# P times V of the 8-key units in 64-key pieces on two row halves of the array

## The chip, the cores and the metric

The kernel runs on one NeuronCore of a Trainium2 chip. The core has a matrix engine (TensorE, "PE" in the profile, with its weight loads as "PEld"), VectorE ("DVE"), ScalarE ("ACT"), GpSimd ("POOL") and SyncE ("SP"); each works through its own instructions in order and waits on semaphores for the others. Matrix products land in PSUM, an accumulator memory of eight banks of 512 floats per partition. The metric is the device time of one execution in microseconds (us), lower is better.

## The reference

Two attention layers work on separate inputs, and their outputs are put side by side. Both have 2048 tokens, width 1024 and 32 heads of 32. Layer B sees the last 256 keys. Layer A sees 8 keys, each two tokens apart:

```python
W, dil = 8, 2
qkv = (x @ wqkv) ...                       # q, k, v of 32 heads
idx = pos[:, None] - off[None, :]          # off = arange(8) * 2
logits = einsum("bhsd,bhswd->bhsw", q, kg) * scale     # masked where idx < 0
o = einsum("bhsw,bhswd->bhsd", softmax(logits), vg)
return o.reshape(B, S, D) @ wo
```

The kernel takes A's even tokens and its odd tokens as two sequences of 1024, in which a query sees itself and the seven keys before it.

## The kernel before, in words

The work is cut into eight units of 512 tokens. Units 0 to 3 are layer B ("dense" in the code), units 4 to 7 are layer A ("window" in the code). Units 1, 2, 3, 5 and 7 continue a sequence, so that they need keys of the unit ahead of them; the code calls this a halo. A unit works through eight groups of four heads. For each group there is the product of the projections q and k (`qk_items`, the matmuls of L576), in some places a product for v (`v_items`, L641), and later the output projection (`o_items`, L702). These are the general matmuls. Each is done in three terms of split operands: a high part and a low part of each float, hence the splitting of weights on ScalarE or VectorE (L216, L219, L222) all through the kernel.

A group of a window unit (`window`, L741) goes through these steps.

1. `scores` (L772): for each of four blocks of 128 keys, for each 64-key half of a block and for each of the four heads, a matmul of 64 keys by 72 queries with a contraction of 32. The outputs go to four PSUM banks of the ring `rs`, one for each head. The item is ready only when all four banks of the ring are free (`rs.empty()`), and when the group two before it is done with its buffers.
2. `mask`, `top`, `expo`, `total` (L780 to L808): softmax on VectorE and ScalarE, in a tile `band`.
3. Transposes in 32 by 32 blocks (L811) and `spread` (L820, L823): ScalarE puts the pieces into a tile `wide`, where each head has, for each block of 128 keys, a stretch of 136 queries. What no key sees there is zero.
4. `values` (L838): P times V. For each block and head a matmul with the 128 keys as contraction, the 32 columns of V as stationary operand, and the 136 queries of the block as moving operand (128 in the last block); with a halo, 8 queries more against the last block of the unit before. Heads go to four quarters of the partitions of one PSUM bank, the only one of the ring `ro`. Blocks overlap in 8 queries and are accumulated there.
5. `finish` (L883): ScalarE copies the bank as the high part of the output (L888), and VectorE later subtracts to get the low part (L892). Then the bank is given back.

The order of all instructions is set when the kernel is built. A planner (`Clock` and the loop at the end of the kernel) keeps an estimated time for each engine. It goes through four lists of items (`aux`, `twos` with second scores and values, `ones` with first scores, `gemm` with the general matmuls) and always issues the one that can start first by these estimates. An item has a ready time, a price in us of TensorE's time, and an `after` that issues the following work of other engines. The price of `scores` is `CW` = 0.75, that of `values` is `C3 + 0.9` = 1.1. Work put off with `ck.defer` is issued when the planned time of TensorE has reached the time given. A ring gives a bank out by `take` and gets it back by `give` with a planned time.

The dense units have their own scores (L923, L1005) and values (L1052); they also end in `finish`.

Of the kernel before, what the change touches and what calls it, by code (L numbers as in the profile page):

```python
# [7 lines left out]
F32 = mybir.dt.float32  # L8
F32R = mybir.dt.float32r
AF = mybir.ActivationFunctionType  # L10
ALU = mybir.AluOpType
# [3 lines left out]
P = 128  # L15
NG = 8
NK = 8
S = 512
# [8 lines left out]
LAG7, LAG0 = 1, 3  # L27
TAIL = 4
C1, C3, CG, CV = 0.108, 0.2, 0.231, 0.242
CW = 0.75  # L30
ORDER = (0, 1, 2, 3, 4, 5, 6, 7)
PACE = ((0.1, 1.2, 0.1, 0.0, 0.0, -99, 2), (0.2, 1.2, 0.0, 0.0, 0.2, -99, 1), (0.2, 1.2, 0.0, 0.0, 0.0, -99, 2), (0.2, 0.6, 0.0, 0.0, 0.2, -99, 2), (4.0, 7.0, 0.5, 0.0, 1, 2), (4.0, 7.0, 1.5, 0.5, 1, 1), (4.0, 7.0, 0.5, 0.2, 1, 3), (4.0, 7.0, 0.5, 0.0, 1, 2))
V_AT = ({1: 0, 3: 1, 7: 2}, {0: 0, 5: 1, 7: 2}, {0: 0, 5: 1, 7: 2}, {0: 0, 5: 1, 7: 2}, {0: 0, 5: 1, 7: 2}, {0: 0, 6: 1, 7: 2}, {0: 0, 5: 1, 7: 2}, {0: 0, 5: 1, 7: 2})
# [210 lines left out]
def kernel(ctx, tc, xs, wqk, wv, wo, outs, units):  # L244


    nc = tc.nc
# [17 lines left out]
    ck = Clock()  # L265


    def parts_of(u):
        return VPARTS if len(V_AT[u]) == 3 else VPARTS_LATER
# [40 lines left out]
    for p in plan:  # L310
# [3 lines left out]
        elif p[0] == "v":  # L314
            if slots_of(p[1]).get(NG - 1) == p[2] and p[1] + 1 < U:
                continue
            s0, n = parts_of(p[1])[p[2]]
# [10 lines left out]
        else:  # L328
            u = p[1] - 1
# [8 lines left out]
    for key, i in where.items():  # L338
        u = min(key[1] + (key[0] == "o"), U - 1)
# [3 lines left out]
    st = Stream(nc, ck, raws, wpool, xpool, items, [more[:, 1024 * i:1024 * i + 1024] for i in range(3)],  # L343
                light)
# [65 lines left out]
    band, wide, turned = [None, None], [None, None], [None, None]  # L410
# [3 lines left out]
    xt, xready, ot, rows = {}, {}, {}, {}  # L414
    done, waiting = {}, {}
# [26 lines left out]
    rg, rs, ro = Ring(psg, 7 - NS, "g"), Ring(pss, NS, "s"), Ring(pso, 1, "o")  # L442
# [7 lines left out]
    def latest(*ts):  # L450
        return None if any(t is None for t in ts) else max(ts)
# [278 lines left out]
    def x_items(u):  # L730
        xt[u], xready[u] = [], []

        def run(g):
            a, b = st.get(where["x", u, g])
            xt[u] += a
            xready[u] += b

        return [[(lambda: 0.0, lambda g=g: run(g), 0.0, lambda: None)] for g in range(4)]


    def window(u, s):  # L741


        has_halo = units[u][3]
        buf = s % 2
        hg = u * NG + s
        vp, vc = vparts[parts_of(u)][s]
        v = vbufs[parts_of(u)][vp]
# [4 lines left out]
        def p16():  # L753
            return band[buf][:, :1536].rearrange("p (i c) -> p i c", c=96)[:, :, 24:]

        kbs = [(-1, 0, 8)] if has_halo else []
        kbs += [(0, 0, 136), (1, 128, 136), (2, 256, 136), (3, 384, 128)]
        h = {}

        def scores_ready():  # L760
# [67 lines left out]
        def values_ready():  # L828
            if st.next_holds() is not None and (st.next_holds(), NG - 1) not in done["out"]:
                return None  # L830
            return latest(done["v"].get((u, vp)), h.get("p"), ro.when())

        def values():
            h["o"], _ = ro.take()
            for n, (kb, q0, w) in enumerate(kbs):
                c = 136 * kb + 8 if kb >= 0 else 0
                for j in range(4):
                    nc.tensor.matmul(h["o"][32 * j:32 * j + 32, q0:q0 + w],  # L838
                                     v[:, (4 * u + kb) % 6, vc + 32 * j:vc + 32 * j + 32], wide[buf][:, j, c:c + w],
                                     start=(n == 0), stop=(n == len(kbs) - 1), skip_group_check=True)  # L840

            def after():
                finish(u, s, h)

            return after

        return [Item(scores_ready, scores, CW)], [Item(values_ready, values, C3 + 0.9)]

    def free_keys(hg):

# [32 lines left out]
    def finish(u, s, h):  # L883
        hg = u * NG + s
        done["o"][hg] = ck.now
        o = st.tile(u)
        ot[u, s] = o
        nc.scalar.copy(o[:, 0, :], h["o"])  # L888
        r = ck.use("act", 0.485, ck.now + ck.SEM)

        def low():
            nc.vector.tensor_tensor(o[:, 1, :], h["o"], o[:, 0, :].bitcast(F32), op=ALU.subtract)  # L892
            e = ck.use("dve", 0.61, r)
            ro.give(0, e)
            done["ot"][hg] = e

        ck.defer(r, low)


    def attention(u, s):  # L900
        dense, has_halo = units[u][2], units[u][3]
        if not dense:
            return window(u, s)
# [174 lines left out]
    for u in range(U):  # L1078
        for s in range(NG):
            a, b = attention(u, s)  # L1080
# [15 lines left out]
    for p in plan:  # L1096
        if p[0] == "qk":
            new = qk_items(p[1], p[2])
            if p == ("qk", 0, 0):
                q, k, x = new[:NK], new[NK:], x_items(0)  # L1100
# [16 lines left out]
    n = TAIL  # L1117
# [11 lines left out]
    if WARM:  # L1129
        idle = qst[1][:, 0, :]  # L1130
        nc.vector.memset(idle.bitcast(F32), 0.0)
        ps, bank = rs.take()
# [77 lines left out]
```

## Time and profile before

| | |
|---|---|
| timed runs | 1805.52, 1805.71 and 1807.08 us |
| median of them | 1805.71 us |
| profiled execution, first to last instruction (span) | 1803.3 us |
| TensorE busy | 1788.7 us (99%) |
| VectorE busy | 1229.5 us (68%) |
| ScalarE busy | 1036.7 us (57%) |
| GpSimd busy | 386.9 us (21%) |
| granted TensorE clock | 1.000 |

The profiled execution is known by its span; the timed runs are 2.2 to 3.8 us longer than it. In the profile's lists, a group of instructions is named by its line in the kernel, its engine and operation, the tile written and the tile read, and the shape. Behind the count stand the busy time of the group, the mean duration of one in ns, and the idle time of the engine just ahead of them with what ended it. The ends of matmuls are modelled, and matmuls overlap each other, so what an item takes of TensorE is better read from starts: from its first matmul to the first matmul of the next item. A matmul of plain floats stands as two records.

### The profile page before, as it was taken

The numbers are of one execution on the slowest core, as the hardware profiler recorded it, in microseconds if no ns is written. First come the engines' busy times: TensorE is split into PE (matmuls) and PEld (weight loads), VectorE is DVE, ScalarE is ACT, GpSimd is POOL, SyncE is SP. The second block draws the span as 40 slices with busy tenths as digits, with TensorE's granted clock in tenths as the row PEclk, the third lists the DMA queues.
The fourth block names the chain that finished last, engine by engine and source line by source line (L and its number), as shares of the span: only waits on it lengthen the run. The fifth ranks groups of instructions, "written<-read, shape, count | busy, mean of one in ns | idle before, by whom it ended". The sixth has DMA issues, their size and how long they took to land.

```text
span 1803.3 us, 34584 instructions
## 1 busy us (share of the span) xinstructions
PE 1788.7 (99%) x12778; PEld 1462.7 (81%) x12778; DVE 1229.5 (68%) x2631; ACT 1036.7 (57%) x2643; POOL 386.9 (21%) x905
## 2 busy tenths in 40 slices
PE   8999999999999999999999999999999999999999
PEld 6787877888787788787888788878888888888887
DVE  6677875657766668666676486686677566866673
ACT  5667667665766665766677364453445344634452
POOL 3222223232232223323233300110001100100000
PEclk9999999999999999999999999999999999999999
DMA  8355665545546455554544433433334443533332
GB/s 243 115 151 136 184 167 148 170 130 172 160 135 177 139 152 176 139 155 134 153 137 138 128 125 125 140 126 135 128 112 151 142 135 113 159 129 135 126 105 82
DMA packets 109129, 257.20 MB, mean 143 GB/s; under 512 B 14496, under 2 KB 29856, under 8 KB 108960
## 3 DMA queue, kind: packets, MB, share of 16 engines
q0 software_dynamic: 41760, 152.06, 26.6%
q1 hardware_dynamic: 56832, 83.00, 17.3%
q10 hardware_dynamic: 10368, 19.93, 3.0%
q8 instruction: 101, 1.65, 0.4%
q14 instruction: 68, 0.56, 0.1%
HBM read 164.63 MB, written 23.07 MB: 104 GB/s over the span
## 4 chain that ended last, share of the span: by engine, by line
PE 94%; DMA 2%; ACT 2%; DVE 2%; issue 0%; POOL 0%; ACTq 0%; SPq 0%; DVEq 0%
PE g L576 38%; PE g L702 19%; PE g L641 18%; PE s L1005 6%; PE s L923 5%; PE o L1052 5%; PE o L838 2%; PE s L772 1%; DMA kst<-nat 1%; DMA halo<-nat 1%; ACT qst L968 1%; DVE s L928 0%; DVE w L222 0%; DMA raw<-xs 0%; ACT kst L391 0%; DMA qst<-nat 0%
## 5 line engine op out<-in xcount | busy, mean ns | idle before, releaser
L576 PE MATMUL g<-x,w 128*128 128x512 f32 x3072 | 763.7, 393 | 2.4 <-ACT x L216 1.3
L576 PEld LDWEIGHTS g<-x,w 128*128 128x128 f32 x3072 | 567.1, 188 | 111.5 <-issue 3.2
L641 PE MATMUL g<-w,x 128*128 128x256 f32 (+1 forms) x2304 | 390.0, 320 | 1.3 <-DVE w L222 1.2
L928 DVE CUSTOM_DVE_ANT_0 s<-s,mask_d 128x384 f32<-128x384 f32 (+2 forms) x512 | 263.2, 553 | 153.5 <-PE s L923 152.3
L222 DVE TENSOR_TENSOR w<-raw,w 128x512 fp32r<-128x512 f32 x516 | 336.6, 694 | 41.1 <-ACT w L216 34.6
L641 PEld LDWEIGHTS g<-w,x 128*128 128x128 f32 x2304 | 333.0, 190 | 30.6 <-DVE w L222 3.2
L702 PE MATMUL g<-ot,w 128*128 128x512 f32 x1416 | 344.0, 393 | 0.9 <-ACT ot L888 0.7
L933 ACT ACTIVATE s<-s,nm 128x384 f32<-128x384 f32 (+2 forms) x512 | 273.5, 535 | 75.0 <-DVE nm L928 72.7
L702 PEld LDWEIGHTS g<-ot,w 128*128 128x128 f32 x1416 | 261.8, 188 | 56.1 <-issue 1.8
L991 POOL TENSOR_SCALAR_AFFINE_SELECT pbuf<-pbuf 128x128 f32<-128x128 f32 (+1 forms) x574 | 205.9, 386 | 267.7 <-ACT pbuf L1012 263.7
L1012 ACT ACTIVATE pbuf<-s 128x384 f32<-128x384 f32 (+2 forms) x480 | 199.5, 506 | 54.7 <-PE s L1005 51.7
L219 DVE CAST w<-raw 128x1024 fp32r<-128x1024 f32 x189 | 130.8, 692 | 76.7 <-PE g L576 44.4
L166 POOL DMA_DIRECT2D raw<-wqk x126 | 68.7, 545 | 458.9 <-DVE w L222 315.8
L923 PE MATMUL s<-kst,qst 96*128 96x384 f32 (+2 forms) x512 | 144.5, 342 | 2.2 <-DMA kst<-nat 1.8
L1005 PEld LDWEIGHTS s<-qst,kst 128*128 128x128 f32 x704 | 108.9, 189 | 36.0 <-ACT s L933 13.2
L1005 PE MATMUL s<-qst,kst 128*128 128x256 f32 (+2 forms) x704 | 132.1, 303 | 1.4 <-ACT qst L968 1.0
L820 ACT COPY wide<-wide 32x256 f32<-32x256 f32 x256 | 103.4, 404 | 38.3 <-DVE wide L811 34.9
L923 PEld LDWEIGHTS s<-kst,qst 96*128 96x128 f32 x512 | 92.4, 188 | 27.2 <-issue 8.1
L166 POOL DMA_DIRECT2D raw<-wv x72 | 46.4, 644 | 279.7 <-DVE w L222 167.9
L933 ACT ACTIVATION_READ_ACCUMULATOR s<-s,nm 128x1 f32 x512 | 104.7, 205 | 0.2
L166 POOL DMA_DIRECT2D raw<-wo x64 | 36.1, 564 | 295.2 <-DVE w L222 158.2
L594 ACT COPY ost<-g 128x512 f32<-128x512 f32 x44 | 25.8, 586 | 120.2 <-PE g L702 120.2
(79 smaller groups left out, 1399.4 us busy)
## 6 DMA issues: line engine op xcount, KB each, us to landing
raw<-wqk POOLq DMA_DIRECT2D x126, 512.0 KB, 3.7
raw<-wv POOLq DMA_DIRECT2D x72, 512.0 KB, 4.2
raw<-wo POOLq DMA_DIRECT2D x64, 512.0 KB, 3.9
qst<-nat SPq DMA_DIRECT2D x96, 256.0 KB, 3.8
kst<-nat SPq DMA_DIRECT2D x96, 256.0 KB, 4.0
raw<-xs POOLq DMA_DIRECT2D x28, 512.0 KB, 4.5
outs<-ost ACTq DMA_DIRECT2D x56, 256.0 KB, 2.2
kst<-halo SPq DMA_DIRECT2D x72, 128.0 KB, 2.7
```

The lines of the kernel that those rows point to most:

```text
L166: (self.nc.scalar if early else self.nc.gpsimd).dma_start(raw if len(ap.shape) == 2 else raw.rearrange("p (a b) -> p a b", a=2), ap)
L219: nc.vector.tensor_copy(t[:, 0, :], raw)
L222: nc.vector.tensor_tensor(t[:, 1, c:c + 512], raw[:, c:c + 512], t[:, 0, c:c + 512].bitcast(F32), op=ALU.subtract)
L576: nc.tensor.matmul(h["ps"], h["w"][:, a, k * P:(k + 1) * P], xt[u][k][:, b, :], start=(k == 0 and i == 0), stop=(k == NK - 1 and i == 2))
L641: nc.tensor.matmul(ps, xt[u][kw * g + k][:, a, p0:p0 + P], h["w"][g][:, c, k], start=(first and t == 0 and half == 0), stop=(last and t == 2),
L702: nc.tensor.matmul(h["ps"], w[:, a, c:c + P], ot[u, k][:, b, :], start=(k == 0 and i == 0), stop=(k == NK - 1 and i == 2))
L923: nc.tensor.matmul(ps[:, :n], q[0:96, j, b * P:(b + 1) * P], kk[0:96, j, c0:c1], start=True, stop=True)
L928: nc.vector.tensor_tensor_reduce(ps[:, :n], ps[:, :n], mask[:, cut:full], scale=-1.0, scalar=BIG, op0=ALU.add, op1=ALU.min, accum_out=nm)
L933: nc.scalar.activation(ps[:, :n], ps[:, :n], AF.Exp, bias=nm, scale=-1.0, accum_out=sm)
L991: nc.gpsimd.affine_select(w, w, pattern=[[0, m], [step, n]], compare_op=ALU.is_ge, fill=0.0, base=base, channel_multiplier=chan)
L1005: nc.tensor.matmul(ps[:, i * n:(i + 1) * n], kk[:, j, 256 + kb * P:256 + (kb + 1) * P], q[:, j, q0:q0 + n], start=True, stop=True)
L1012: nc.scalar.activation(w, ps[:, :pack * n].rearrange("p (j n) -> p j n", j=pack), AF.Exp)
```

## The change

Only units 4 to 7 are edited. In `values` each 128-key block is taken in two pieces of 64 keys. A piece is a matmul with a contraction of 64, on the lower or the upper 64 rows of the array, with 72 queries as moving operand (64 for the last piece). The lower pieces are accumulated in the bank of `ro`, as before; the upper pieces go to a second bank, one of the four of the ring `rs`, which `values` now waits for and takes. A halo is one more piece of 8 queries for each head on the upper rows.

Every bank holds 72 queries of each 128, so the two banks overlap in 8 queries of each 64. A new `join` takes the place of `finish`: ScalarE copies the first 8 columns of every 64 of the upper bank to an unused part of `band`; VectorE adds them to the lower bank; ScalarE copies columns 72 to 127 of each 128 from the upper bank and columns 0 to 71 from the lower one as the high part; VectorE subtracts, later, in the same two portions. The upper bank is given back after the first subtraction, the lower one after the second. The planned price of `values` is now `C3 + CP` = 0.7.

```diff
-CW = 0.75
+CW, CP = 0.75, 0.5
...
-            return latest(done["v"].get((u, vp)), h.get("p"), ro.when())
+            return latest(done["v"].get((u, vp)), h.get("p"), ro.when(), rs.when())
 
         def values():
             h["o"], _ = ro.take()
-            for n, (kb, q0, w) in enumerate(kbs):
-                c = 136 * kb + 8 if kb >= 0 else 0
+            h["o2"], bank = rs.take()
+            halves = [h["o"], h["o2"]]
+            blocks = [(-1, 1, 0, 8)] if has_halo else []
+            blocks += [(b, i, P * b + 64 * i, min(72, S - P * b - 64 * i)) for b in range(4) for i in range(2)]
+            seen = set()
+            for b, i, q0, w in blocks:
+                c = 136 * b + 8 + 64 * i if b >= 0 else 0
+                r = slice(64 * i, 64 * i + 64)
                 for j in range(4):
-                    nc.tensor.matmul(h["o"][32 * j:32 * j + 32, q0:q0 + w],
-                                     v[:, (4 * u + kb) % 6, vc + 32 * j:vc + 32 * j + 32], wide[buf][:, j, c:c + w],
-                                     start=(n == 0), stop=(n == len(kbs) - 1), skip_group_check=True)
+                    nc.tensor.matmul(halves[i][32 * j:32 * j + 32, q0:q0 + w],
+                                     v[r, (4 * u + b) % 6, vc + 32 * j:vc + 32 * j + 32], wide[buf][r, j, c:c + w],
+                                     start=(i, j) not in seen, stop=True, skip_group_check=True)
+                    seen.add((i, j))
 
             def after():
-                finish(u, s, h)
+                join(u, s, h, bank, 0 if has_halo else 1)
...
-        return [Item(scores_ready, scores, CW)], [Item(values_ready, values, C3 + 0.9)]
+        return [Item(scores_ready, scores, CW)], [Item(values_ready, values, C3 + CP)]
...
+    def join(u, s, h, bank, first):
+        hg = u * NG + s
+        done["o"][hg] = ck.now
+        o = st.tile(u)
+        ot[u, s] = o
+        lower, upper = [x.rearrange("p (n c) -> p n c", c=64) for x in (h["o"], h["o2"])]
+        low, high = [[x.rearrange("p (b c) -> p b c", c=P)[:, :, c0:c1] for x in (h["o"], h["o2"], o[:, 0, :], o[:, 1, :])]
+                     for c0, c1 in ((0, 72), (72, P))]
+        over = band[s % 2][:, 1536:1600].rearrange("p (n c) -> p n c", c=8)[:, first:]
+        nc.scalar.copy(over, upper[:, first:, :8])
+        e = ck.use("act", 0.2, ck.now + ck.SEM)
+        nc.vector.tensor_tensor(lower[:, first:, :8], lower[:, first:, :8], over, op=ALU.add)
+        e = ck.use("dve", 0.22, e)
+        nc.scalar.copy(high[2], high[1])
+        ck.use("act", 0.35, ck.now)
+        nc.scalar.copy(low[2], low[0])
+        r = ck.use("act", 0.4, e)
+
+        def lows():
+            nc.vector.tensor_tensor(high[3], high[1], high[2].bitcast(F32), op=ALU.subtract)
+            e = ck.use("dve", 0.38, r)
+            rs.give(bank, e)
+            nc.vector.tensor_tensor(low[3], low[0], low[2].bitcast(F32), op=ALU.subtract)
+            e = ck.use("dve", 0.45, r)
+            ro.give(0, e)
+            done["ot"][hg] = e
+
+        ck.defer(r, lows)
```

More of the change, by code (lines that the diff above doesn't have):

```diff
@@ L754, in p16 @@
             return band[buf][:, :1536].rearrange("p (i c) -> p i c", c=96)[:, :, 24:]
-        kbs = [(-1, 0, 8)] if has_halo else []
-        kbs += [(0, 0, 136), (1, 128, 136), (2, 256, 136), (3, 384, 128)]
         h = {}
```

## The prediction

> **What bounds the kernel now.** I read the page first (busy shares, clock, chain of waits), then the waits and the busy time of the stretch that the change touches, then the groups by shape, then the timeline of TensorE around the changed item.
>
> ```profile
> span 1803.3 us, 34584 instructions
> ...
> PE 1788.7 (99%) x12778; PEld 1462.7 (81%) x12778; DVE 1229.5 (68%) x2631; ACT 1036.7 (57%) x2643; POOL 386.9 (21%) x905
> ...
> PEclk9999999999999999999999999999999999999999
> ...
> PE 94%; DMA 2%; ACT 2%; DVE 2%; issue 0%; POOL 0%; ACTq 0%; SPq 0%; DVEq 0%
> PE g L576 38%; PE g L702 19%; PE g L641 18%; PE s L1005 6%; PE s L923 5%; PE o L1052 5%; PE o L838 2%; PE s L772 1%; DMA kst<-nat 1%; DMA halo<-nat 1%; ACT qst L968 1%; DVE s L928 0%; DVE w L222 0%; DMA raw<-xs 0%; ACT kst L391 0%; DMA qst<-nat 0%
> ```
>
> The chain that sets the end is TensorE for 94% of the span, at full clock. The edited product (L838) is 2% of it. Three more views, a row of each: the product's own line (shortest, median and longest record in ns, first and last start in us); the waits of TensorE from 1053 us to the end, of which this row is the only one; and the busy time by stretch, in the order PE, PEld, DVE, ACT, POOL.
>
> ```profile
> L838 PE MATMUL o<-wide,vbuf x1152: 176/279/303, 1053.6 to 1769.3; 128*32 128x136 f32 x130, 128*32 128x128 f32 x42, 128*32 128x8 f32 x20
> ...
> PE g L641 <- DVE w L222: 0.7, 1, 0.7
> ...
> 1053.00:1773.00 720.00, 719.28 (x6276) 597.91 (x6276) 511.24 (x726) 345.42 (x769) 73.42 (x133) 1.00 0.40 131
> ```
>
> The product runs only in the last four units, so the first 1053 us should come out as they are. From there TensorE waits 0.7 us in all, and VectorE (511.24 of 720) and ScalarE (345.42) have much idle time. So in this stretch a microsecond less on TensorE is a microsecond less of span, as long as the order of the other engines still keeps up with it.
>
> **The change, part 1: the product itself.** The groups by shape, of the lines concerned:
>
> ```profile
> L772 PE MATMUL s<-pbuf 32*64 32x72 f32 x2048 | 30.0, 234 | 0.0
> L838 PE MATMUL o<-wide,vbuf 128*32 128x136 f32 x768 | 29.2, 282 | 0.0
> ...
> L838 PE MATMUL o<-wide,vbuf 128*32 128x128 f32 x256 | 13.4, 273 | 0.0
> ...
> L838 PE MATMUL o<-wide,vbuf 128*32 128x8 f32 x128 | 4.0, 186 | 0.0
> ```
>
> Each written matmul stands in the trace as two records (32 groups x 12 matmuls of 136 columns are 768 records). A group now has 32 records, in sub-arrays of 128 rows by 32 columns, four beside each other; 16 of the 32 groups have eight records more (8 columns, the halo). The busy sums overlap, so what an item takes is read from the timeline, from its first start to the first start of what follows. First the plain item, then one with a halo:
>
> ```profile
> 1053.59 1.12 PE L838 MATMUL o<-wide,vbuf 128*32 128x136 f32 x32
> 1054.64 0.94 PE L772 MATMUL s<-pbuf 32*64 32x72 f32 x64
> 1055.51 1.66 PE L702 MATMUL g<-ot,w 128*128 128x512 f32 x6
> 1057.00 8.33 PE L576 MATMUL g<-x,w 128*128 128x512 f32 x36
> ```
>
> ```profile
> 1338.40 1.18 PE L838 MATMUL o<-wide,vbuf 128*32 128x8 f32 x40
> 1339.52 0.94 PE L772 MATMUL s<-pbuf 32*64 32x72 f32 x64
> 1340.38 5.07 PE L576 MATMUL g<-x,w 128*128 128x512 f32 x21
> ```
>
> Values now: 1054.64 - 1053.59 = 1.05 us plain, 1339.52 - 1338.40 = 1.12 us with halo. After the change a group has 8 pieces x 4 heads x 2 = 64 records of 72 columns (the last of 64), on eight sub-arrays of 64 rows by 32 columns; a halo adds eight, as before. No row shows that sub-array. The nearest is the scores item, L772: also 64 records, also 72 columns, also eight sub-arrays taken in turn, two of the array's sides swapped. It takes 1055.51 - 1054.64 = 0.87 us (0.86 at 1339.52). Bounds: from below, if only streaming counted, eight sets of 136 columns take 1.05, so the work of four times two sets of 72 on either half, side by side, is 1.05 x 72/136 = 0.56 us. From above, if the two halves ran one after the other, twice that, 1.11 us. I take 0.87, because L772 agrees in count, width and number of sub-arrays, and its 0.87 is visibly more than streaming alone: twice the instructions have to be issued. The halo's eight records cost 1.12 - 1.05 = 0.07 now; on L772's average (0.87/64 each) they would cost 0.11; I keep 0.07, so 0.94. Saved: 16 x (1.05 - 0.87) + 16 x (1.12 - 0.94) = **5.8 us**.
>
> A rule speaks against this: the Trainium skill, page "TensorE: Matmul & The Clock Gate", section "Wait — 56ns, not 53.3ns?", says that matmuls never start closer than about 25 ns however small they are. By it 64 records would take at least 1.6 us, an estimate from that page, and the item would get longer by half. The trace disagrees for sub-arrays in turn: L772 averages 0.87/64 = 0.0136 us a record.
>
> **Part 2: values and scores no longer side by side.** Values now take one of the four score banks (`rs`) beside the output bank, and give it back when `join` has read it; `scores` wants all four free. So scores can't follow values at once. They do today in six of 32 groups, the first at 1053.59 (above), the last here (chain of waits from 1700 us):
>
> ```profile
> 1713.01 1.11 PE o L838 x40
> 1714.12 0.87 PE s L772 x53
> ```
>
> Such a pair leaves the full-array form once instead of twice. What leaving costs comes from a long run of full-array matmuls and from the two just ahead of the item at 1053.59:
>
> ```profile
> 1302.52 22.00 PE g L576 x96
> ...
> 1053.05 0.61 PE L702 MATMUL g<-ot,w 128*128 128x512 f32 x2
> ```
>
> The long run has 0.229 us a matmul. Between 1055.51 and 1057.00 above stand six in 1.49, where 1.37 is due: 0.12 on the way back. From 1053.05 to 1053.59 stand two in 0.54: 0.08 on the way in. Six pairs lost x 0.20 = **+1.2 us**. The gap that scores now leave is filled by general matmuls, which were next in any case (L702, L576 in the rows above). If that cover is missing, scores wait on TensorE: that is a rival below. The copies on SP's queue that refill a seat after scores move with them; no DMA is added, and none is moved on POOL's queue.
>
> **Part 3: `join` for `finish`, 32 times.** The rows that price it:
>
> ```profile
> L780 DVE TENSOR_TENSOR band<-s,near 128x288 f32<-128x288 f32 x128 | 49.4, 448 | 39.8 <-PE s L772 39.8
> ...
> L892 DVE TENSOR_TENSOR ot<-o,ot 128x512 fp32r<-128x512 f32 x64 | 43.9, 686 | 69.2 <-ACT ot L888 69.1
> ...
> L888 ACT CAST ot<-o 128x512 fp32r<-128x512 f32 x64 | 37.5, 587 | 98.2 <-PE o L1052 56.1 <-PE o L838 41.6
> ...
> L486 ACT COPY tails<-g 128x8 f32<-128x8 f32 x16 | 2.7, 171 | 0.0
> ```
>
> VectorE: 288 elements take 0.448, 512 take 0.686, so 1.06 ns an element; the three new ones (64, 224, 288 elements) take 0.21 + 0.38 + 0.45 = 1.04 in place of 0.69, +0.35 a group, 11 us in all. ScalarE: 8 elements 0.171, 512 elements 0.587, so 64, 224 and 288 take 0.22 + 0.35 + 0.40 = 0.97 in place of 0.59, +0.38, 12 us in all. Idle in the stretch: 209 us of VectorE, 375 of ScalarE. New waits: VectorE's add stands for ScalarE's small copy, which stands for TensorE's last matmul; ScalarE's lower copy stands for that add. Behind the add queue the weight splits (L222) that TensorE needs next, and the steps of the next softmax; behind the copy ScalarE's casts and the copies into `wide`. VectorE already stands here for ScalarE, and ScalarE for TensorE (waits from 1053 us on):
>
> ```profile
> ACT ot L888 <- PE o L838: 41.6, 27, 3.0
> ...
> DVE ot L892 <- ACT ot L888: 57.2, 18, 5.2
> ```
>
> Both come early to this point and sit over a microsecond. So the sum for TensorE is 0, the cover being that idle time. Without it: up to 0.35 + 0.38 plus about half a microsecond of standing, 1.2 us x 32 = 39 us if all of it reached TensorE, which the idle shares exclude; below nothing it can hardly go, since TensorE waits 0.7 us in all for VectorE.
>
> The output is ready at most about 0.5 us later (ScalarE +0.38, VectorE's last step after it +0.14). Where this is closest is the end:
>
> ```profile
> 1768.28 1.29 PE L838 MATMUL o<-wide,vbuf 128*32 128x8 f32 x40
> ...
> 1769.50 0.96 PE L702 MATMUL g<-ot,w 128*128 128x512 f32 x3
> 1769.62 0.59 ACT L888 CAST ot<-o 128x512 fp32r<-128x512 f32 x1 [1.21 <-PE o L838]
> ...
> 1770.24 0.69 DVE L892 TENSOR_TENSOR ot<-o,ot 128x512 fp32r<-128x512 f32 x1 [2.15 <-ACT ot L888]
> 1770.30 4.95 PE L702 MATMUL s<-ot,x 128*128 128x512 f32 x21
> 1775.09 2.20 PE L702 MATMUL g<-ot,w 128*128 128x512 f32 x9
> ```
>
> The last head group is ready at 1770.93 and first used at 1775.09, when the seven other steps of the four blocks are through: 4.2 us to spare, so 0.5 costs nothing; were it more than 4.2, the rest would be added to the end.
>
> **Part 4: the planner's price.** The item is planned with 0.7 in place of 1.1 us, so every later decision of order may differ. Its price is unknown; TensorE's stalls are small enough today that a new order can hardly gain, and I take 0, with the rival below for a loss.
>
> **Sum.** -5.8 + 1.2 + 0 + 0 = -4.6 us, a span of 1798.7. The page's execution has a span of 1803.3, the median of the three runs is 1805.7, 2.4 us more, which lies outside the first and last instruction and stays. Predicted: 1805.7 - 4.6 = **1801.1 us**, -0.25%. What a measurement of this kernel can tell from no change is about 0.2%, 3.6 us: faster begins at 1802.1, slower at 1809.3.
>
> **The rivals.**
> (a) The halves don't run side by side, so the change doesn't do what it says. Then values take 1.11 and 1.18: +0.06 x 32 = 1.9, with part 2 +3.1, 1808.8 us. For it: no row shows 64-row sub-arrays. Against it: L772 runs eight at once.
> (b) Slower: scores behind `join`. In the six pairs scores become ready only when values are through, so their group is late already; now the planner places them 1.9 us later by its own figures (`join`'s 0.2, 0.22, 0.4 and 0.38 in the diff, and the planner's handovers of 0.2, 0.15, 0.115, 0.15 and 0.115 between them). If general matmuls run out behind this delay, since they need the seats and outputs of such groups, TensorE stands. All six: 11.6 - 4.6 = +7.0, 1812.7 us; it decides (over 3.6) from 4.2 of the six on. The same sum stands for other stalls of a new order. For it: six groups do go straight from values to scores. Against: general matmuls follow each of them in the timeline, and 26 groups have no such pair.
> (c) Records cost what they cost in L838, 1.05/32 = 0.033 us each, however small. Then 64 take 2.1 us: +1.05 x 32 + 1.2 = +35, 1841 us. L772 speaks against it. The page on TensorE named above would have this case in a milder form.
> (d) Streaming alone: 0.56 and 0.63 us, saving 0.49 x 32 = 15.7, with part 2 -14.5, 1791.2 us. Against it: L772 at 0.87.
>
> **How the numbers follow.** Forecast 57% (own range 1798 to 1803.5, of which about a tenth lies within 0.2%), (a) 15%, (b) 20% (partly paid: two in five of it ends within 0.2%), (c) 3%, (d) 5%. Faster: 0.51 of the forecast and 0.05 of (d), 0.56; slower: 0.12 of (b), 0.03 of (c), 0.03 of (a), 0.18; the rest, 0.26, within 0.2%. The range goes down to an item of 0.71 us, halfway to (d) (-0.34 x 32 + 1.2 = -9.7), and up through (a) and about two thirds of (b): 1796 to 1810.
>
> **What would show it.** Right: the values item at about 0.87 and 0.94 us from start to next start, 64 and 72 records; TensorE's chain as before up to 1053 us; no group with scores straight behind values; VectorE about 11 and ScalarE about 12 us busier; no new row among TensorE's waits. Wrong: a values item at 1.1 or more (a), rows of TensorE waiting for `join`'s subtraction or for L222 (b), the item far under 0.87 (d), or a last values item so late that the tail waits for it.

## The result and the profile after

The changed kernel takes 1819.17 us (median of five runs, 1818.61 to 1819.62) against 1806.51 us for the kernel before on the same chip: ratio 1.0071, with a 95% interval of 1.006 to 1.0083. It is 12.7 us slower. The forecast was 4.6 us faster, and the range ended at 1810.

The page of the changed kernel, with the lines that answer to those quoted of before; in it, values are L842 and scores L770:

```profile
span 1817.7 us, 36767 instructions
...
PE 1790.2 (98%) x13802; PEld 1462.1 (80%) x13802; DVE 1239.2 (68%) x2697; ACT 1041.5 (57%) x2705; POOL 387.2 (21%) x905
...
PE 87%; DVE 4%; DMA 3%; ACT 3%; issue 2%; SPq 0%; ACTq 0%; POOL 0%; DVEq 0%; POOLq 0%
```

VectorE is busy for 9.7 us more and ScalarE for 4.8 us more, out of 1818 (the new operations overlap in part; their own durations add up to 12 us more on either engine). The shares look as before. But the chain that sets the end now runs over TensorE for 87% in place of 94%, and the difference went to VectorE, ScalarE, transfers and issue. Who TensorE waits for, from the first scores of the window units to the end (columns: total us, times, longest):

```profile
PE g L641 <- DVE w L222: 5.0, 3, 2.5
PE g L576 <- DVE w L222: 2.9, 1, 2.9
PE g L576 <- ACT w L216: 1.4, 1, 1.4
PE o L842 <- ACT wide L821: 1.3, 2, 0.9
PE s L842 <- ACT wide L821: 1.1, 3, 0.4
PE g L702 <- ACT ot L922: 1.0, 1, 1.0
```

Before, this view had one row of 0.7 us. The waits are for weight splits (L222, L216), for the copies into `wide` (L821), which the product itself needs, and once for `join`'s lower copy (L922). None is for the second bank.

The product did get shorter. In the timeline of TensorE, the plain values item that answers to the one at 1053.59 (the first two rows and the last of its 64 records, and what follows), then the first row of an item with a halo and what follows it:

```profile
1057.10 0.27 PE L842 MATMUL o<-wide,vbuf 64*32 64x72 f32 x4
1057.12 0.27 PE L842 MATMUL s<-wide,vbuf 64*32 64x72 f32 x4
...
1057.70 0.27 PE L842 MATMUL s<-wide,vbuf 64*32 64x64 f32 x4
1057.90 1.66 PE L702 MATMUL g<-ot,w 128*128 128x512 f32 x6
```

```profile
1255.62 0.21 PE L842 MATMUL s<-wide,vbuf 64*32 64x8 f32 x4
...
1256.46 3.02 PE L702 MATMUL g<-ot,w 128*128 128x512 f32 x12
```

0.80 us in place of 1.05, and 0.84 in place of 1.12. Both halves, `o` and `s`, start within 0.02 us of each other: the row halves run side by side.

Where the time went can be summed from the starts of TensorE's records, from each item's first start to the next item's, from the first scores on. Values: 35.3 us before, 31.8 after; they would be 26.3 if all items were as undisturbed as the two above. L576: 329.1, 337.9. L641: 161.3, 166.2. Scores: 27.7, 28.1. L702: 181.6, 181.9. Together +10.9 us, so the general matmuls stand for 14 us more and the values items give back 5.5 of the 9.0 that they would have won. The other 3.5 us between the two profiled executions lie ahead of the first scores, where both kernels have the same instructions; most of that is the clock at the start (6.8 us at half speed, told of at the end).

One of these waits, read in the timeline of the changed kernel:

```profile
1385.15 0.23 DVE L918 TENSOR_TENSOR o<-o,band 128x64 f32<-128x64 f32 x1
1385.41 0.40 ACT L922 CAST ot<-o 128x288 fp32r<-128x288 f32 x1 [3.32 <-DVE o L918]
1385.71 1.17 ACT L794 ACTIVATE band<-band 128x1152 f32<-128x1152 f32 x1
...
1387.52 0.45 DVE L929 TENSOR_TENSOR ot<-o,ot 128x288 fp32r<-128x288 f32 x1
1387.90 1.34 DVE L802 TENSOR_REDUCE sm<-band 128x16 f32<-128x1152 f32 x1
...
1392.72 1.25 DVE L222 TENSOR_TENSOR w<-raw,w 128x512 fp32r<-128x512 f32 x2
...
1394.03 1.20 PE L641 MATMUL g<-w,x 128*128 128x512 f32 x4 [2.53 <-DVE w L222]
```

ScalarE has stood 3.32 us for the add of `join` (L918), which lay behind other work in VectorE's line. But that is not what TensorE stands for here: the exponential behind ScalarE's copy (L794) ends at 1386.88, and VectorE takes up the step that needs it (L802) only at 1387.90. From 1381.29 on VectorE has no gap in its line. It is full, with `join`'s add and its two subtractions (0.23, 0.39 and 0.45 us) and a softmax ahead of the weight's subtraction (L222), and TensorE stands 2.53 us for that.

The longest wait, 2.85 us at 1176.6, has nothing of `join` just ahead of it: no operation of `join` is in VectorE's line from 1160 us up to there. VectorE stood 2.96 and 0.80 us there for casts of x by ScalarE (L216), and ScalarE 3.90 and 3.11 us for the transfers of x ahead of these casts. So the changed kernel's waits mix work, standing in line and a new order, and the experiments have to tell them apart.

### The profile page after: what moved, and what is told of

The parts are those of the page before. It is cut to its first block, busy times and chain, and to the rows that moved or that the text cites. A ratio compares the mean times of both kernels' runs of the same rounds, so it can differ in the third digit from the quotient of the medians.

```text
span 1817.7 us, 36767 instructions
## 1 busy us (share of the span) xinstructions
PE 1790.2 (98%) x13802; PEld 1462.1 (80%) x13802; DVE 1239.2 (68%) x2697; ACT 1041.5 (57%) x2705; POOL 387.2 (21%) x905
## 4 chain that ended last, share of the span: by engine, by line
PE 87%; DVE 4%; DMA 3%; ACT 3%; issue 2%; SPq 0%; ACTq 0%; POOL 0%; DVEq 0%; POOLq 0%
PE g L576 36%; PE g L702 19%; PE g L641 15%; PE s L1041 5%; PE s L959 5%; PE o L1088 5%; DMA raw<-xs 1%; PE s L770 1%; DVE w L222 1%; PE s L842 1%; DMA kst<-nat 1%; PE o L842 1%; ACT wide L818 1%; ACT qst L1004 1%; DMA raw<-wv 0%
## 5 line engine op out<-in xcount | busy, mean ns | idle before, releaser
L576 PE MATMUL g<-x,w 128*128 128x512 f32 x3072 | 771.7, 395 | 6.4 <-DVE w L222 3.0
L576 PEld LDWEIGHTS g<-x,w 128*128 128x128 f32 x3072 | 570.4, 189 | 116.6 <-DVE w L222 5.2
L641 PE MATMUL g<-w,x 128*128 128x256 f32 (+1 forms) x2304 | 390.2, 321 | 5.7 <-DVE w L222 5.5
L222 DVE TENSOR_TENSOR w<-raw,w 128x512 fp32r<-128x512 f32 x516 | 336.5, 694 | 38.3 <-ACT w L216 31.7
L641 PEld LDWEIGHTS g<-w,x 128*128 128x128 f32 x2304 | 333.0, 190 | 35.1 <-DVE w L222 8.0
L702 PE MATMUL g<-ot,w 128*128 128x512 f32 x1416 | 344.4, 394 | 1.9 <-ACT ot L922 1.0
L702 PEld LDWEIGHTS g<-ot,w 128*128 128x128 f32 x1416 | 262.1, 188 | 55.8 <-ACT ot L922 1.2
L959 PEld LDWEIGHTS s<-kst,qst 96*128 96x128 f32 x512 | 92.6, 189 | 28.1 <-issue 9.1
L1088 PE MATMUL o<-pbuf,vbuf 128*32 128x384 f32 (+2 forms) x1408 | 91.9, 389 | 0.0
```

The costliest lines, as they stand in the source:

```text
L222: nc.vector.tensor_tensor(t[:, 1, c:c + 512], raw[:, c:c + 512], t[:, 0, c:c + 512].bitcast(F32), op=ALU.subtract)
L576: nc.tensor.matmul(h["ps"], h["w"][:, a, k * P:(k + 1) * P], xt[u][k][:, b, :], start=(k == 0 and i == 0), stop=(k == NK - 1 and i == 2))
L641: nc.tensor.matmul(ps, xt[u][kw * g + k][:, a, p0:p0 + P], h["w"][g][:, c, k], start=(first and t == 0 and half == 0), stop=(last and t == 2),
L702: nc.tensor.matmul(h["ps"], w[:, a, c:c + P], ot[u, k][:, b, :], start=(k == 0 and i == 0), stop=(k == NK - 1 and i == 2))
L959: nc.tensor.matmul(ps[:, :n], q[0:96, j, b * P:(b + 1) * P], kk[0:96, j, c0:c1], start=True, stop=True)
L1088: nc.tensor.matmul(h["o"][32 * j:32 * j + 32, q0:q0 + n], v[:, slot, vc + 32 * j:vc + 32 * j + 32], pbuf[:, j, at[ki]:at[ki] + n], start=( ...
```

## The experiments

Three theories stand behind the first expectations. J: `join` holds back weight splits and copies. P: the planner's price of 0.7 us spoils the order. R: any new order loses by chance. Later J was cut into the work that `join` adds (JV, later V) and the waits between engines that it makes (JW, later W), and R and P became one, the order (O), against the operations whatever the order (D). Each result is the median, with the ratio to the kernel before on the same chip and its 95% interval. The kernel before had medians of 1806.4 to 1807.1 us in these comparisons. A gain or loss in us is the difference of two medians; the intervals reach about 2 to 3 us to either side, and for e9 the ratio would give +9.8 us where the medians give +8.0.

### Price and join, each alone

`e1_price11`, on the changed kernel:

```diff
-CW, CP = 0.75, 0.5
+CW, CP = 0.75, 0.9
```

> The changed kernel with the planner's price of values put back from 0.7 to 1.1 us (CP 0.9). Theory J (join: its steps on ScalarE and VectorE, and the add that ScalarE stands for, hold back weight splits and the copies into wide): the stalls stay, 1815 to 1823 us. Theory P (the price of 0.7 makes the planner choose a bad order): most stalls go, 1799 to 1806 us. Theory R (any new order loses by chance against one that was chosen by trial): anything between 1802 and 1822, with stalls at other places than in the changed kernel.

Measured 1822.35 us, 1.0085 (1.007 to 1.01). The price is not what the changed kernel lost by; P falls.

`e2_before_price07`, on the kernel before:

```diff
-        ... values_ready, values, C3 + 0.9
+        ... values_ready, values, C3 + 0.5
```

> The kernel before, with the planner's price of values alone lowered from 1.1 to 0.7 us; the same instructions in another order. J: within 0.2% of before, 1803 to 1810 us. P: slower by most of what the change lost, 1814 to 1822 us. R: slower by 3 to 10 us.

Measured 1810.1 us, 1.0018 (1.0009 to 1.0028). The same instructions in another order cost 3.3 us, at the low end of what R said. The prediction had put 0 on it.

`e3_no_join`, on the changed kernel (64 columns of each 128 of the lower bank are read twice):

```diff
-                join(u, s, h, bank, 0 if has_halo else 1)
+                rs.give(bank, ck.now)
+                finish(u, s, h, True)
...
+            src = src.rearrange("p (b c) -> p b c", c=P)[:, :, None, :64].to_broadcast([P, 4, 2, 64])
```

> The changed kernel with its pieces in two banks and the price of 0.7, but without join: finish reads 64 columns of each 128 of the lower bank twice (same number of elements as before, one instruction each on ScalarE and VectorE), the upper bank is not read and is given back at once. The output leaves out the upper half of the keys. J: the product's gain of about 9 us comes through, 1796 to 1801 us. P: 1812 to 1820 us, since the price is the same. R: 1800 to 1815 us.

Measured 1805.6 us, 0.9998 (0.9989 to 1.0008). Without `join` 13.6 us of the changed kernel's time are gone, as J said; but the product's gain of 9 us doesn't come through either, so J's range is missed.

`e4_join_alone`, on the kernel before, with `join` reading and writing the one output bank:

```diff
-                finish(u, s, h)
+                join(u, s, h, 0 if has_halo else 1)
```

> The kernel before, its product and its price of 1.1 kept, with join's five operations in place of finish, all on the one output bank (the eight columns are added to themselves, so the output differs there). J: slower by more than the change, since the product gains nothing: 1815 to 1828 us. P: within 0.3% of before, 1803 to 1811 us. R: 1806 to 1818 us.

Measured 1821.34 us, 1.0087 (1.0072 to 1.0102). `join` alone costs at least as much as the whole change. J holds, for `join` together with the order that its prices bring.

### Work or wait

`e5_join_deferred`, on the changed kernel:

```diff
+        def add():
+            nc.vector.tensor_tensor(lower[:, first:, :8], lower[:, first:, :8], over, op=ALU.add)
+            e1 = ck.use("dve", 0.22, e0)
+            ck.defer(r, highs)
+            ck.defer(e1, copy)
...
+        ck.defer(e0, add)
```

> The changed kernel with join's operations kept, each issued only at the planned time at which its input is ready: the copy of eight columns and the upper copy at once, the add when that copy is done, the upper subtraction and the lower copy after the add, the lower subtraction last. Same work, the same price of 0.7, other order. Theory JW (join's harm is the standing in line: VectorE at the add for ScalarE and TensorE, ScalarE at the lower copy for the add): most stalls go, 1799 to 1807 us. Theory JV (its harm is the work that it adds to VectorE and ScalarE, 0.35 and 0.38 us a group): 1814 to 1822 us as the change.

Measured 1825.44 us, 1.0097 (1.0082 to 1.0112): a miss for JW, 6 us worse than the change, and above JV's range too. Deferring made yet another order, with other waits, among them these two (waits of TensorE):

```profile
PE g L576 <- DVE w L222: 4.7, 2, 3.3
PE g L702 <- DVE ot L937: 4.5, 1, 4.5
```

`e8_deferred_price11` is the same with `CP` at 0.9.

> As e5_join_deferred with the planner's price of values at 1.1 in place of 0.7 us. JW: 1799 to 1808 us, within 4 us of e5_join_deferred. JV: 1814 to 1823 us.

Measured 1821.56 us, 1.008 (1.0065 to 1.0095), a miss for JW too; it is in JV's range.

`e6_work_alone`, on the kernel before:

```diff
-        nc.scalar.copy(o[:, 0, :], h["o"])
+        nc.scalar.copy(spare, h["o"].rearrange("p (n c) -> p n c", c=64)[:, :, :8])
+        nc.scalar.copy(high[1], high[0])
+        nc.scalar.copy(low[1], low[0])
...
+            nc.vector.tensor_tensor(extra, h["o"]..., cst["near"]..., op=ALU.add)
+            nc.vector.tensor_tensor(high[2], high[0], high[1].bitcast(F32), op=ALU.subtract)
+            nc.vector.tensor_tensor(low[2], low[0], low[1].bitcast(F32), op=ALU.subtract)
```

> The kernel before with its product and price, where finish is split in join's portions (two copies, two subtractions) and has an extra copy and an extra add of 64 elements that nobody waits for; the work of join without its wait between engines. The output stays the reference's. JW: 1805 to 1810 us. JV: 1815 to 1825 us, as join alone (1821.3).

Measured 1812.26 us, 1.0029 (1.002 to 1.0039): between the two theories.

`e7_add_alone`, on the kernel before:

```diff
+        nc.scalar.copy(over, lower[:, :, :8])
+        e = ck.use("act", 0.2, ck.now + ck.SEM)
+        nc.vector.tensor_tensor(lower[:, :, :8], lower[:, :, :8], over, op=ALU.add)
+        e = ck.use("dve", 0.22, e)
         nc.scalar.copy(o[:, 0, :], h["o"])
```

> The kernel before with its product and price, one copy and one subtraction as in finish, and ahead of them the copy of eight columns and the add on VectorE for which ScalarE's copy stands (the eight columns are added to themselves, so the output differs there). Less work than join (+0.21 ScalarE, +0.23 VectorE a group) and all of its wait. JW: 1815 to 1825 us. JV: 1808 to 1813 us.

Measured 1815.64 us, 1.0049 (1.0032 to 1.0066), at the low end of JW: the wait costs more than the work, but all of these runs also change the order, which e2 had priced at 3 us for nothing.

### The same with the order of before held

The next kernels let the planner count `join` as `finish` and values at 1.1 us, so that, except for e10, TensorE, SP and POOL get the very order of before, and ScalarE and VectorE too except for the replaced operations.

`e9_join_frozen`, on e4_join_alone:

```diff
-        e = ck.use("act", 0.2, ck.now + ck.SEM)
...
-        r = ck.use("act", 0.4, e)
+        r = ck.use("act", 0.485, ck.now + ck.SEM)
...
-            e = ck.use("dve", 0.38, r)
...
-            e = ck.use("dve", 0.45, r)
+            e = ck.use("dve", 0.61, r)
```

> The kernel before with its product and price and with join's five operations on the one output bank, as e4_join_alone, but the planner still counts them as finish's one copy and one subtraction; so TensorE, SP and POOL have the very order of before, and ScalarE and VectorE too except for the replaced operations (the eight columns are added to themselves, so the output differs there). Theory O (the loss is in the new order that the planner makes of everything behind it): 1806 to 1811 us. Theory D (the operations and their waits cost this whatever the order): 1817 to 1825 us, as join alone (1821.3).

Measured 1815.11 us, 1.0054 (1.0039 to 1.0069): +8.0 us, between O and D. Of the 14.6 us of join alone, 8 remain in the old order and about 6 came with the new one. What the 8 are made of, in its waits (TensorE's first, then ScalarE's and VectorE's at `join`):

```profile
PE g L641 <- DVE w L222: 3.8, 2, 2.3
PE o L838 <- ACT vbuf L594: 1.1, 1, 1.1
...
ACT ot L913 <- DVE o L912: 17.3, 32, 3.8
...
DVE o L912 <- ACT band L911: 59.1, 23, 4.7
```

ScalarE stands for the add in all 32 groups. VectorE's 59.1 us are about what it had at `finish` (57.2), only now the standing begins ahead of the add, with more behind it.

`e11_work_frozen` is e6_work_alone counted in the same way.

> As e6_work_alone (before, finish in join's portions with an extra copy and an extra add that nobody waits for; the output stays the reference's), planned as finish, so that the order is the one of before. O: 1805 to 1808 us. D: 1810 to 1814 us, as work alone (1812.3).

Measured 1807.38 us, 1.0005 (0.9995 to 1.0014). `join`'s amount of work, with nobody standing and nothing moved, costs nothing that can be told from no change (the interval ends at 2.5 us). So nearly all of e6's 5.3 us was order.

`e14_dve_stands` and `e15_act_stands`, on the kernel before, each with one small pair of operations at the head of `finish`:

```diff
+        nc.scalar.copy(over.rearrange("p (n c) -> p n c", c=8), h["o"]...)     # e14: VectorE stands for ScalarE
+        nc.vector.tensor_tensor(sums, over, near, op=ALU.add)
...
+        nc.vector.tensor_tensor(sums, near, near, op=ALU.add)                  # e15: ScalarE stands for VectorE
+        nc.scalar.copy(over, sums)
```

> The kernel before in its own order, its finish kept; added are a copy of eight columns of each 64 on ScalarE at the end of values and, at the same place of VectorE's line, an add of 64 elements of that copy, whose result nobody reads. So VectorE stands for ScalarE and TensorE there, and ScalarE stands for nobody. If VectorE's standing is what cost 8 us in e9: 1812 to 1817 us. If ScalarE's is: 1806 to 1809 us.

> The kernel before in its own order, its finish kept; added are an add of 64 constant elements on VectorE, which waits for nobody, and ahead of finish's copy a copy of the sum on ScalarE, which stands for it in VectorE's line. If ScalarE's standing is what cost 8 us in e9: 1811 to 1817 us. If VectorE's is: 1806 to 1809 us.

Measured 1810.85 us, 1.0024 (1.0014 to 1.0035), and 1810.3 us, 1.002 (1.0011 to 1.0029): +4.0 and +3.4. Neither is the one cause; both cost, and their sum, 7.4, is about e9's 8.0. (From the first scores to the end, summed by TensorE's starts as above, the profiles have +3.0, +4.1 and +7.8, and +1.2 for e11.) In both, TensorE waits longer for the weight split, 2.7 us in e14 and 3.0 in e15, where the kernel before has 0.7 and e11 1.6:

```profile
PE g L641 <- DVE w L222: 2.7, 2, 2.3
```

```profile
PE g L641 <- DVE w L222: 3.0, 2, 2.2
```

Here the way from the standing to TensorE can be followed. First the kernel before, then the same place in e14:

```profile
1183.73 1.35 DVE L804 TENSOR_REDUCE sm<-band 128x16 f32<-128x1152 f32 x1 [0.96 <-ACT band L796]
1190.46 3.47 PE L641 MATMUL g<-w,x 128*128 128x512 f32 x14 [0.72 <-DVE w L222]
```

```profile
1186.56 0.22 DVE L909 TENSOR_TENSOR band<-band,near 128x64 f32<-128x64 f32 x1 [2.40 <-ACT band L908]
1192.10 1.27 DVE L222 TENSOR_TENSOR w<-raw,w 128x512 fp32r<-128x512 f32 x2
1193.43 3.48 PE L641 MATMUL g<-w,x 128*128 128x512 f32 x14 [2.26 <-DVE w L222]
```

In e14 VectorE's add (L909) lies ahead of the softmax step L804 and stands until ScalarE has copied from the values product. Before, L804 started 0.03 us behind the values item of TensorE (1183.70); in e14 it starts 1.57 us behind it (1186.70 against 1185.13). The weight's subtraction (L222), further on in the same line, comes later by as much, and TensorE's wait grows by the same 1.54 us. In e15, at a place where TensorE does not stand before and stands 0.65 us in e11, it is ScalarE:

```profile
1570.36 0.25 ACT L909 COPY band<-band 128x64 f32<-128x64 f32 x1 [4.15 <-DVE band L908]
1571.48 1.05 ACT L216 CAST w<-raw 128x1024 fp32r<-128x1024 f32 x1
1572.56 1.30 DVE L222 TENSOR_TENSOR w<-raw,w 128x512 fp32r<-128x512 f32 x2 [0.74 <-ACT w L216]
1579.90 2.34 PE L641 MATMUL g<-w,x 128*128 128x512 f32 x9 [2.23 <-DVE w L222]
```

The cast of a weight (L216) lies behind the standing copy, VectorE stands for that cast, and TensorE for what VectorE does next.

`e13_pieces_frozen` is e3_no_join with the figures of before.

> As e3_no_join (the upper half of the keys is left out of the output), but planned with the figures of before, so that TensorE has the order of before. W: the product's gain comes through, 1796 to 1800 us. If the gain is lost to something else than the order, 1803 to 1807 us as e3_no_join.

Measured 1803.99 us, 0.9979 (0.997 to 0.9989): -2.9 us, a miss for W. It is in the range of the other theory, that the gain is lost to something else than the order: in the order of before, and without any of `join`, only a third of the product's gain of 9.0 comes through. By TensorE's starts, values take 27.5 us in place of 35.3, but scores 30.3 in place of 27.7, and L641 162.6 in place of 161.3; with the rest it is -3.6 in all. Scores lose in two ways. The item at 1385.72 takes 1.1 us more than 0.87, since it stops for a transfer into `pbuf`. And the six scores straight behind values are longer than 0.87; the first of them takes 1058.13 - 1057.08 = 1.05:

```profile
1057.08 1.12 PE L770 MATMUL s<-pbuf 32*64 32x72 f32 x64
1058.13 1.65 PE L702 MATMUL g<-ot,w 128*128 128x512 f32 x6
```

The six lie between 1.05 and 1.21 us, 1.5 us more in sum than six of 0.865.

`e10_after_finish_prices` is the changed kernel, counted with the figures of before; the second bank still moves scores, and with them the order.

> The changed kernel, its pieces, second bank and join all kept, planned with the figures of before: values at 1.1 us, join as one copy of 0.485 and one subtraction of 0.61. Only the second bank, for which scores wait, still moves the order. O: 1799 to 1808 us. D: 1813 to 1822 us.

Measured 1827.06 us, 1.0111 (1.0094 to 1.0128), a miss for O and above D's range: the worst of all, with this row, among others, in TensorE's waits, which is the wait of scores for `join`'s upper subtraction:

```profile
PE s L770 <- DVE ot L923: 2.5, 3, 1.7
```

`e12_no_pingpong` and `e16_vector_join` are attempts at a whole kernel in the order of before. In e12 ScalarE makes four copies that wait for nobody, and VectorE does the rest later:

```diff
+        nc.scalar.copy(low_hi[:, :, 8:64], low[:, :, 8:64])
+        nc.scalar.copy(high_hi, high)
+        nc.scalar.copy(up, high)
+        nc.scalar.copy(over, upper[:, first:, :8])
+        rs.give(bank, ck.now)
```

> The pieces in two banks with another join, in the very order of before (TensorE, SP and POOL have it in full): planned as finish and with values at 1.1 us, and the second bank counted as free at once. ScalarE makes four copies when values are through, none of which waits for VectorE: the middle 56 columns of the lower half, the upper half's 56 as high part and once more as they are, and the eight overlapping columns. VectorE does the rest at the place where it did the subtraction of before: add, copy of the eight columns, two subtractions. More work than join (about +0.67 ScalarE, +0.57 VectorE a group over finish). The output stays the reference's. Theory W (what costs is waiting between engines and the new order, not work): 1797 to 1803 us. Theory V (work on ScalarE and VectorE costs): 1808 to 1820 us.

Measured 1813.97 us, 1.0033 (1.002 to 1.0047), a miss for W. In the six pairs scores stand for ScalarE's last copy, and the weight split is late again:

```profile
PE s L770 <- ACT band L922: 4.5, 6, 1.5
PE g L641 <- DVE w L222: 3.4, 2, 1.8
```

In e16 the first two copies are VectorE's:

```diff
-        nc.scalar.copy(low_hi[:, :, 8:64], low[:, :, 8:64])
-        nc.scalar.copy(high_hi, high)
...
+            nc.vector.tensor_copy(low_hi, low)
...
+            nc.vector.tensor_copy(high_hi, up)
```

> As e12_no_pingpong, in the order of before, with other shares: ScalarE only copies the upper half's 56 columns and the eight overlapping ones (about 0.56 us, as finish's copy), so the second bank is free after two copies in place of four; VectorE does the add, both high parts and both subtractions at the place of finish's subtraction, about 1.2 us a group more than finish, 39 us in all. The output stays the reference's. If work on VectorE is covered by its idle time (209 us in the stretch of before): 1803 to 1808 us. If it is not: 1812 to 1825 us.

Measured 1814.93 us, 1.0046 (1.0029 to 1.0063), 1.9 us of scores' waits and 4.5 for the split:

```profile
PE g L641 <- DVE w L222: 4.5, 2, 2.3
PE s L770 <- ACT band L920: 1.9, 5, 1.1
```

VectorE is busy for 1261.3 us here, 31.8 more than before; so much is not covered, though the 5.7 more of e11 (1235.2) were. How the 8.6 us of loss divide between this work and the second bank was not tested. No version with the whole output beat the kernel before.

### What they add up to

In the order of before, pieces without `join` are worth -2.9 us (e13) and `join`'s operations cost +8.0 (e9), of which the two standings are 4.0 and 3.4 alone (e14, e15) and the work about nothing (e11). That is +5.1; the change measured +12.7. The 7.6 between are what is left for the new order, by subtraction and not by a run of its own, so that they are uncertain by some 4 us; a new order alone cost 3.3 (e2), 4.9 (e6 less e11) and 6.2 us (e4 less e9) where it could be told apart. The operations of the change itself, in four other orders, lost 14.6 to 20.0 us (e1, e5, e8, e10), so the order moves the whole change by 7 us too. What pieces and `join` cost only together, through the second bank that `join` holds and scores need, is in the 7.6 as well: no run has this `join` on two banks in the order of before.

## Why the prediction was wrong

- **What bounds the kernel.** "A microsecond less on TensorE is a microsecond less of span, as long as the order of the other engines still keeps up with it": the condition didn't hold. e13 took 7.8 us from the values items and got 2.9: weight splits (1.3) and a transfer (1.1) came no earlier, and the scores behind values got longer (1.5). The idle 209 us of VectorE and 375 of ScalarE are standing in line, for TensorE most of all, not time that can be filled at will; and where weights for the next unit and for v are split (1176 to 1196, 1340 to 1395, 1570 to 1600 us) VectorE was idle for 11 to 21% of the time, against 29% on average. In the kernel before, VectorE is busy for 52.82 of the 65 us here:

```profile
1335.00:1400.00 65.00, 65.00 (x656) 54.66 (x655) 52.82 (x76) 36.82 (x82) 8.44 (x14) 1.00 0.41 131
```

- **Part 1, the product.** The mechanism was right, the size too small: 5.8 us forecast, 9.0 measured on undisturbed items (16 x 0.25 + 16 x 0.28 = 8.5, and 0.5 of stalls that the old items had). The scores item was a good measure, the piece is a little faster still: 0.80 against 0.87. The rule of 25 ns between starts, of the Trainium skill's page "TensorE: Matmul & The Clock Gate", section "Wait — 56ns, not 53.3ns?", disagrees with this trace as it did with the scores: 0.80/64 is 0.0125 us a record.
- **Part 2, the pairs.** All six are gone in the changed kernel, as said. Their price of 1.2 us was not measured by itself; e13 shows that keeping them would not have been worth that, since scores behind 64-record values lose 1.5 us in six.
- **Part 3, `join`: the step that failed.** The operations take what was forecast: the add 0.22 to 0.23, the copies 0.21, 0.35 and 0.40, the subtractions 0.385 and 0.45. That this work is covered is right for its amount (e11, within its interval). "So the sum for TensorE is 0, the cover being that idle time" is wrong for its waits, which cost 8.0 us (e9). The prediction named them, and what is queued behind, and then held the engine's mean idle time against them; but an engine that stands in line holds back what lies behind it, whatever its mean. In e15 ScalarE stood 4.15 us for an operation of 0.22, and TensorE 2.23 us behind it. That VectorE comes early to this point was an average too: the row quoted for it has 18 waits for 32 groups, so in the other 14 VectorE did not stand there.
- **Part 3, the end.** The reserve held. The last head group, whose values item starts at 1782.29 in the changed kernel, is ready at 1785.46 and first used at 1789.47, so 4.0 us are left. What lost was the group before it, which the prediction did not look at: its values item at 1768.56 takes 3.7 us to the next item's start, since it was issued ahead of the last copies into `wide`, and 1.0 of the 3.7 is TensorE standing for `join`'s lower copy (the last row of TensorE's waits above).
- **Part 4, the order: the second step that failed.** "I take 0" is short by about 7.6 us (by subtraction, above). TensorE's order is the same up to the first values item, as said, and differs from the next item on.
- **The rivals.** (a) falls, the halves run side by side. (b)'s own mechanism, scores behind `join`, did not decide: no row of TensorE's waits shows it in the changed kernel; it shows in e10, with 2.5 us. Its last sentence, "other stalls of a new order", is half of what happened; it had 20% and came to 7.0 us slower in all, where 12.7 were measured although the product won more than forecast. The sign set down for it, TensorE standing for L222, did come. (c) and (d) did not happen.

## What to carry to other kernels

Idle time of a helper engine is no cover for an operation that makes the engine stand in line; ask, for each new wait, what is behind it and when the critical engine needs that, in the busiest stretch and not on average. When a greedy planner writes the order, hold the old order fixed first (same prices, other instructions): here that told the cost of the work (nothing), of its waits (8 us) and of the new order (3 to 6 us) apart. Time taken from the critical engine comes through only where what it needs next is ready earlier too: 7.8 us shorter items gave 2.9.

## What the runs showed of the hardware

Two row halves of 64 by four column quarters run side by side at 0.0125 us a record, which is as good as the eight sub-arrays of scores. But two such items of 64 records in a row slow the second from 0.87 to 1.05 us and more (e13); no run shows why.

The clock of TensorE can fall within the kernel after a stall. Busy time by stretch in the changed kernel, the start and a stretch behind the 2.85 us wait at 1176.6 to 1179.5 us; the last three columns are granted clock, DMA share and GB/s:

```profile
0.00:40.00 40.00, 35.11 (x130) 26.97 (x131) 22.88 (x50) 22.23 (x46) 14.64 (x43) 0.91 0.75 233
1181.00:1184.00 3.00, 3.00 (x8) 2.34 (x8) 2.96 (x8) 2.40 (x8) 1.04 (x2) 0.50 0.61 197
```

Half clock lasted 3.4 us there, so the stall of 2.9 us cost about 1.7 more. At the start it lasted 6.8 us, and 3.4 in most of the other kernels' profiles; the quoted profile of the kernel before had none, which by these lengths makes its execution about 3.4 us better at the start than the changed kernel's and 1.7 us better than most. In e5 the waits were followed by 17 us of half clock in all (8.5 us lost), which is part of why long waits cost more than they last. The length of a wait does not decide it alone: one of 2.5 us in the changed kernel (from 1391.5), one of 3.0 in e4 (from 1191.0) and one of 2.3 in e9 (from 1193.2) were not followed by any, while one of 1.4 us in e1 (from 1349.8) was. The Trainium skill's page "TensorE: Matmul & The Clock Gate", section "What's actually happening", gives a window of about 3.4 us in which the activity of the engine is judged; the trace agrees on the length of the half-clock stretches, while waits shorter than that were enough to start one, 2.85 us in the changed kernel.
